# A causal convolution fused with a multiplicative FFN: where two convolution heads stand among the products, and who sums the band matrices

## The chip, the cores and the metric

The kernel runs on 1 core of one Trainium2 chip. The metric is the device time of one execution in microseconds (us). An execution is profiled once, and the trace of that execution is what is read here; times are also taken without the profiler, and their median is the kernel's time. TensorE is called PE (its weight loads PEld), VectorE DVE, ScalarE ACT, GpSimd POOL, SyncE SP.

## What is computed

`x` is (8, 3904, 192). Each of the 8 heads owns 24 of the 192 channels and has 7 taps, a softmax over its row of `weight`. The convolution is causal: output row s is the weighted sum of rows s-6 to s. Its 31232 rows then go through a multiplicative FFN without a nonlinearity:

```python
out_conv = np.einsum('hk,bskhg->bshg', softmax(weight), x_unfolded)
a = x @ w1            # 192 -> 1024
b = x @ w2            # 192 -> 1024
h = a * b @ w3        # 1024 -> 1024
return h @ w_out      # 1024 -> 192
```

## The kernel before

**Two streams.** The rows are cut into two halves of 15616 rows (`NS = 2`), which lie side by side on partitions 0-63 and 64-127. A *round* is 512 rows of each half (`CH = 512`); there are 31 rounds.

**The convolution** (`conv`, L237) works on windows of 64 rows of which 58 are output rows. A window's product with a 64x64 band matrix (`Aband`, seven diagonals that hold a head's taps) is one matmul in a 64x64 tile of PE; four such tiles run side by side. A *block* is up to 36 windows; there are 10 (`SIZES`). A call with `nh = 1` makes one head of one block: two rows of four matmuls into one PSUM buffer (`cps`), which DVE or ACT then copies to `convo`. Blocks 3 to 9 are stored to DRAM (`rows`) and come back as `xT` through transposing DMAs on SP's queue; blocks 0 to 2 are transposed on PE. `conv_two` (L480) makes two heads, with one copying engine each, and calls `store` after the last head.

**The first product** (`first_product`, L345) makes, for each of 8 tiles `ft` of 128 hidden columns, `pa` (x @ w1) and `pb` (x @ w2): six matmuls each, in 64x128 tiles of PE, two side by side. ACT copies `pa` to `asb` (L366), DVE multiplies `asb` by `pb` into `abT` (L367).

**The second product** (`second_product`, L372) multiplies a round's `abT` with `W_sb` = w3 @ w_out (made once, L405 to L420) in 32 matmuls of 128x128 tiles; ACT copies the result (L383), SP stores it. It runs two rounds behind the first.

**PSUM** is one pool of four buffers of two banks (L65). `pa`, `pb`, `cps`, `ops` and the rest take them in turn, so each allocation takes the buffer of the fourth one before it and waits until that one's reader is done.

**The order is written out by hand** (`manual_schedule`, L67); every engine runs its instructions in program order. After a prologue there are 15 phases (L507). Phase 0 has no first product; each later one has two rounds of first product, then two rounds of second product of two halves each: `ops00`, `ops01`, `ops10`, `ops11`. In phases 0 to 11 four heads of a block are made as well: two between `ops00` and `ops01`, two between `ops10` and `ops11`, all copied by DVE (L521). A block thus takes two phases; the even phase makes heads 0 to 3, the odd one heads 4 to 7.

**The prologue** (L135 to L462) loads x and weights, and makes the bands. POOL makes a mask `cmask` (L151), DVE multiplies it by the taps into `cprod` (128 x 2 x 64 x 8, L206), adds the eight taps up in three steps (L213, L216) and copies the two halves of partitions across (L221, with ACT). PE runs 28 dummy matmuls meanwhile (`warm`, L174), then block 0's heads, its transposes and the first round. `wsw` holds the FFN's weights with the two halves of partitions swapped; `swap_w` (L334) makes it in three column parts (0-511, 512-767, 768-1023) for each of three tiles. Part 0 must be there before the first round's `ft` 0, part 1 before `ft` 4, part 2 before `ft` 6. POOL's queue carries the loads of x, w1, w2, w3 and w_out in program order, between its own work.

Of the kernel before, what the change touches and what calls it, by code (L numbers as in the profile page):

```python
# [8 lines left out]

FP32 = mybir.dt.float32  # L10
BF16 = mybir.dt.bfloat16
AX = mybir.AxisListType
ALU = mybir.AluOpType
# [4 lines left out]
def kernel(  # L18
# [10 lines left out]
    nc = tc.nc  # L29

    B, S, D = x.shape
    H, K = weight.shape
# [4 lines left out]
    KP = 8  # L37
    assert K <= KP

    NS = 2  # L40
# [5 lines left out]
    Q = 64  # L46
# [7 lines left out]
    NB = len(SIZES)  # L54
# [7 lines left out]
    const = ctx.enter_context(tc.tile_pool(name="const", bufs=1))  # L62
# [6 lines left out]
    def banks(name):  # L69
        return psum.tile([128, NS, CH], FP32, tag="banks", name=name)  # L70
# [74 lines left out]

    ones = const.tile([128, 1], BF16)
    nc.gpsimd.memset(ones, 1.0)
    cmask = const.tile([128, Q, KP], BF16)
    for r in range(NS):
        ps = slice(Q * r, Q * r + Q)  # L150
        nc.gpsimd.affine_select(  # L151
            out=cmask[ps], in_=ones[ps].unsqueeze(2).to_broadcast([Q, Q, KP]),
            pattern=[[-1, Q], [-1, KP]], compare_op=ALU.is_equal,
            fill=0.0, base=0, channel_multiplier=1)
    wn = [const.tile([128, DFF], BF16, name=f"wn{k}", tag=f"wn{k}") for k in range(3)]
    wsw = [const.tile([128, DFF], BF16, name=f"ws{k}", tag=f"ws{k}") for k in range(3)]

    WC = (0, DFF // 2, DFF * 3 // 4, DFF)

    def load_w(c0, c1):  # L160
        cs = slice(c0, c1)
        nc.gpsimd.dma_start(out=wn[0][:, cs], in_=moe_w1[0:128, cs])
        nc.gpsimd.dma_start(out=wn[2][0:Q, cs], in_=moe_w1[128:192, cs])
        nc.gpsimd.dma_start(out=wn[2][Q:128, cs], in_=moe_w2[128:192, cs])
        nc.gpsimd.dma_start(out=wn[1][:, cs], in_=moe_w2[0:128, cs])

    load_w(0, WC[2])
    ident = const.tile([128, 128], BF16)
    make_identity(nc, ident)

    def warm(n, t=None):
        t = banks("warm") if t is None else t
        for j in range(n):
            nc.tensor.matmul(t[:, j % 2, :], zeros[:, 0:128], zeros, start=True, stop=True)  # L174

    warm(28)


    wmax = const.tile([128, H], FP32)
# [1 line left out]
    wsb = const.tile([128, 2, 2, KP], BF16)  # L181
# [3 lines left out]
        out=wall, in0=wall, in1=wmax.unsqueeze(2).to_broadcast([128, H, K]), op=ALU.subtract)  # L185
# [3 lines left out]
    for r in range(NS):  # L189
        ps = slice(Q * r, Q * r + Q)  # L190
        nc.vector.tensor_tensor(
            out=wsb[ps, :, :, 0:K],
            in0=wall[ps].rearrange("p (g a e) k -> p g a e k", g=2, a=2)[:, :, r],
            in1=wsum[ps].rearrange("p (g a e) -> p g a e", g=2, a=2)[:, :, r].unsqueeze(3)
                .to_broadcast([Q, 2, 2, K]),
            op=ALU.mult)

    Aband = const.tile([128, 2, 2, 2, Q], BF16)
# [2 lines left out]
        g, j, e = h // 4, (h % 4) // 2, h % 2  # L201
        return Aband[Q * r:Q * r + Q, g, int(j != r), e, :]

    def band(g):
        c = slot([128, 2, Q, KP], BF16, "cprod")
        nc.vector.tensor_tensor(  # L206
            out=c,
            in0=cmask.unsqueeze(1).to_broadcast([128, 2, Q, KP]),
            in1=wsb[:, g].unsqueeze(2).to_broadcast([128, 2, Q, KP]),
            op=ALU.mult)  # L210
        n = KP // 2
        while n > 1:
            nc.vector.tensor_tensor(out=c[:, :, :, 0:n], in0=c[:, :, :, 0:n],  # L213
                                    in1=c[:, :, :, n:2 * n], op=ALU.add)
            n //= 2
        nc.vector.tensor_tensor(out=Aband[:, g, 0], in0=c[:, :, :, 0], in1=c[:, :, :, 1],  # L216
                                op=ALU.add)

    def band_swap(g, half, f):
        d, e = ((Q, 0), (0, Q))[half]  # L220
        f(out=Aband[d:d + Q, g, 1], in_=Aband[e:e + Q, g, 0])  # L221


    xT = [const.tile([128, RING], BF16, name=f"xT{k}", tag=f"xT{k}") for k in range(NP)]
# [12 lines left out]
    def conv(b, h0, nh, evict=None, lead=0):  # L237
        n = SIZES[b] // 2
        if h0 == 0:
            convo_of[b] = work.tile([128, n, NP, NS, Q], BF16, tag="convo", bufs=2, name="convo")  # L240
        convo = convo_of[b]
        cps = banks("cps")
        warm(lead, cps)
        wd = nh * G

        def view(ps, r):
            return cps[ps, r, 0:n * wd].rearrange("p (w g) -> p w g", g=wd)

        for j in range(nh):
            h = h0 + j  # L250
            for c in range(2):
                xb, w0 = xb_of[b][c]
                for r in range(NS):
                    nc.tensor.matmul(  # L254
                        view(slice(Q * c, Q * c + Q), r)[:, :, j * G:(j + 1) * G],
                        band_of(h, r),
                        xb[Q * r:Q * r + Q, w0:w0 + n, h * G:(h + 1) * G],
                        start=True, stop=True)
        src = cps[:, :, 0:n * wd].rearrange("p r (w g) -> p r w g", g=wd)
        o, moves = 0, []  # L260
        for k, c0, m in segments(h0 * G, wd):
            moves.append((convo[:, :, k, :, c0:c0 + m].rearrange("p w r g -> p r w g"),
                          src[:, :, :, o:o + m]))
            o += m
        if h0 + nh == H:
            del xb_of[b]
        if evict == ():
            return moves
        for e, (dst, part) in enumerate(moves):
            f = evict or [nc.scalar.copy]  # L270
            f[e % len(f)](out=dst, in_=part)  # L271
# [28 lines left out]
    def pe_transpose(b, k, lead=0):  # L300
        n = SIZES[b] // 2
        convo = convo_of[b]
        tps = banks_bf16("tps")
        for w in range(lead):
            nc.tensor.transpose(out=tps[:, w % 2, :], in_=zeros[:, 0:128], identity=ident)
        for w in range(n):
            nc.tensor.transpose(  # L307
                out=tps[:, w, :],
                in_=convo[:, w, k].rearrange("p r g -> p (r g)"), identity=ident)
        t0 = tok(FIRST[b])  # L310
        dst = xT[k][:, t0:t0 + 2 * n * ST].rearrange("p (c w s) -> p c w s", c=2, w=n)
        src = tps[:, 0:n, :].rearrange("p w (c s) -> p c w s", c=2)
        return dst, src[:, :, :, 0:ST]
# [20 lines left out]
    def swap_w(k, part, engines):  # L334
        cs = slice(WC[part], WC[part + 1])
        for f, (d, e) in zip(engines, ((0, Q), (Q, 0))):
            f(out=wsw[k][d:d + Q, cs], in_=wn[k][e:e + Q, cs])
# [85 lines left out]
    V, A, P = nc.vector.tensor_copy, nc.scalar.copy, nc.gpsimd.tensor_copy  # L423
# [3 lines left out]
    def move(f, pair):  # L427
        f(out=pair[0], in_=pair[1])  # L428

    band(0)  # L430
    band_swap(0, 0, V)
    band_swap(0, 1, A)
    band(1)
    band_swap(1, 0, V)
    m0, m1 = conv(0, 0, 4, ())
    move(A, m0)
    band_swap(1, 1, A)
    move(V, m1)
    t0 = pe_transpose(0, 0, 10)
    swap_w(0, 0, (V, A))  # L440
    for m in conv(0, 4, 2, ()):
        move(V, m)
    for m in conv(0, 6, 2, ()):
        move(A, m)
    move(V, t0)
    swap_w(2, 0, (V, A))
    t1 = pe_transpose(0, 1, 8)
    move(V, t1)
    t2 = pe_transpose(0, 2)
    move(A, t2)  # L450
    swap_w(1, 0, (V, A))
    for k in (0, 2, 1):
        swap_w(k, 1, (P, V))
    load_w(WC[2], WC[3])
    load_x(2)
    for k in (0, 2, 1):
        swap_w(k, 2, (P, P))
    load_wo()
# [5 lines left out]
    def seq(*fs):  # L464
        def run():
            for f, *a in fs:
                f(*a)
        return run

    first_product(0, lead=2, between={  # L470
        2: seq((conv, 1, 0, 4)),
        3: seq((conv, 1, 4, 4)),
        6: seq((pe_transposes, 1))})
    first_product(1, {
        0: seq((conv, 2, 0, 4)),
# [4 lines left out]
    def conv_two(b, h, engines):  # L480
        for j, f in enumerate(engines):
            conv(b, h + j, 1, (f,))
        if h + 2 == H:
            store(b)

    def send(last):
        while sent[0] <= last and min((sent[0] + 1) * CH, TS) <= stored[0]:
            transposes(sent[0])
            sent[0] += 1
# [16 lines left out]
    done = 0  # L506
    for p, rounds in enumerate(phases):  # L507
        b, e = PROLOGUE_BLOCKS + p // 2, p % 2
        if b < NB:
            for xb, r, w in zero_rows.pop(b, []):  # L510
                nc.gpsimd.memset(xb[Q * r:Q * r + PAD, w, :], 0.0)
        for j, R in enumerate(rounds):
            first_product(R)
            if j == 0 and b + 1 < NB:
                P(out=pace, in_=abT_of[R][0:1, JT - 1, 1, 0:2])  # L515
                load_x(b + 1, (0, 1) if p == 1 else (e,))
        last = NR if p == len(phases) - 1 else done + 2
        for i in range(done, last):
            second_product(i, 0)
            if b < NB and i < done + 2:  # L520
                conv_two(b, 4 * e + 2 * (i - done), (V, V))  # L521
            second_product(i, 1)
        done = last
        send(min(NR - 1, LAG + 2 * p + 4))
    assert sent[0] == NR

# [29 lines left out]
```

## Time and profile before

| | |
|---|---|
| median of 3 runs | 532.54 us (532.4 to 532.62) |
| the profiled execution | 533.68 us, its span 532.0 us |
| PE busy | 524.0 us (98% of the span) |
| DVE, ACT, POOL busy | 363.1 us, 317.4 us, 53.0 us |
| chain that ended last | PE 94%, DVE 3%, ACT 1%, DMA 1% |
| first product, L360 | 59% of the span on that chain |
| second product, L378 | 31% |
| convolution heads, L254 | 2% |
| first matmul of round 0 | 14.02 us after the span's start |
| a phase with heads | 106.8 to 139.5 us (first product to 127.6) |
| a phase without heads | 464.9 to 496.5 us |

The span is the time from the first to the last instruction of the trace; the rest of an execution's time lies around it. A group of instructions has its line in the source, its engine, its operation and its tiles (`out<-in`). Waits are given with the engine that waits and the instruction that ended the wait. The matmuls of one row of tiles run side by side, so the distance from one start to the next, and not their own lengths, tells what PE needs for them.

### The profile page before, as it was taken

To read this page: it belongs to the slowest core of one execution; us is meant where nothing else is said; L and a number is where in the kernel's file an instruction comes from. 1 tells how busy PE (TensorE), PEld (TensorE's weight loads), DVE (VectorE), ACT (ScalarE), POOL (GpSimd) and SP (SyncE) were. 2 spreads that over 40 slices of the span, in tenths; PEclk is the share of its full clock that TensorE was granted. 3 is DMA by queue.
4 is the path that set the end of the run, shared out by engine and by line. 5 is a ranking of instruction groups with operands and counts; after the bars stand their busy time and mean duration, and the time that the engine had idled before them with its cause. 6 is when DMAs were issued, how large, how long until landed. Compare 5 with 4: busy or idle time off the path is not lost.

```text
span 532.0 us, 12708 instructions
## 1 busy us (share of the span) xinstructions
PE 524.0 (98%) x5469; PEld 339.3 (64%) x5469; DVE 363.1 (68%) x350; ACT 317.4 (60%) x350; POOL 53.0 (10%) x95
## 2 busy tenths in 40 slices
PE   8999999999999999999999999999999999999995
PEld 4455874846658476584765757557575674847685
DVE  6779459578594875949669496784957849286560
ACT  3888647375573755737467374664746647375552
POOL 8851002002010100201001010020000000000000
PEclk9999999999999999999999999999999999999998
DMA  7999457989473694637956468655624065240203
GB/s 101 141 206 182 93 96 171 206 175 125 132 99 99 154 144 129 88 103 156 137 139 78 130 150 128 118 66 145 136 80 120 1 172 106 90 76 31 90 22 130
DMA packets 130541, 63.13 MB, mean 119 GB/s; under 512 B 83352, under 2 KB 129460, under 8 KB 130484
## 3 DMA queue, kind: packets, MB, share of 16 engines
q1 hardware_dynamic: 91764, 45.65, 35.7%
q0 software_dynamic: 38576, 16.63, 26.3%
q8 instruction: 43, 0.70, 0.6%
q14 instruction: 14, 0.11, 0.1%
q10 hardware_dynamic: 144, 0.03, 0.0%
HBM read 33.28 MB, written 34.82 MB: 128 GB/s over the span
## 4 chain that ended last, share of the span: by engine, by line
PE 94%; DVE 3%; ACT 1%; DMA 1%; issue 0%; ACTq 0%; DVEq 0%
PE ops L378 31%; PE pa L360 30%; PE pb L360 29%; PE cps L254 2%; DVE abT L367 1%; PE wps L418 1%; ACT asb L366 1%; DMA wall<-in_weight_dram 1%; PE tps L307 1%; PE w3ps L409 0%; DVE cprod L213 0%; DVE cprod L206 0%; DVE Aband L216 0%; DVE convo L428 0%; DVE w3T L412 0%
## 5 line engine op out<-in xcount | busy, mean ns | idle before, releaser
L367 DVE TENSOR_TENSOR abT<-asb,pb 128x1024 bf16<-128x1024 bf16 (+1 forms) x248 | 298.4, 1204 | 77.0 <-ACT asb L366 60.5
L366 ACT CAST asb<-pa 128x1024 bf16<-128x1024 f32 (+1 forms) x248 | 247.6, 999 | 64.1 <-PE pa L360 63.4
L360 PE MATMUL pb<-xT,wn 64*128 64x512 bf16 (+1 forms) x744 | 199.7, 373 | 0.2
L360 PE MATMUL pa<-xT,wn 64*128 64x512 bf16 (+1 forms) x744 | 197.8, 373 | 0.4
L360 PE MATMUL pa<-xT,ws 64*128 64x512 bf16 (+1 forms) x744 | 197.9, 373 | 0.0
L360 PE MATMUL pb<-xT,ws 64*128 64x512 bf16 (+1 forms) x744 | 195.7, 373 | 0.0
L360 PEld LDWEIGHTS <-wn 64*128 64x128 bf16 x1488 | 138.3, 94 | 84.6 <-issue 2.6
L360 PEld LDWEIGHTS <-ws 64*128 64x128 bf16 x1488 | 130.3, 94 | 72.0 <-issue 1.4
L378 PEld LDWEIGHTS <-abT 128*128 128x128 bf16 x1952 | 159.1, 98 | 13.8 <-issue 13.8
L378 PE MATMUL ops<-W_sb,abT 128*128 128x192 bf16 x1952 | 167.8, 246 | 0.0
L383 ACT COPY osb<-ops 128x768 f32<-128x768 f32 (+1 forms) x62 | 48.9, 789 | 134.1 <-PE ops L378 134.1
L271 DVE CAST convo<-cps 128x864 bf16<-128x864 f32 (+7 forms) x65 | 52.0, 847 | 66.7 <-PE cps L254 66.7
L111 POOL DMA_DIRECT2D xb<-in_x_dram x38 | 29.9, 797 | 12.2 <-DMA w3b<-in_moe_w_dram 5.2
L515 POOL COPY pace<-abT 1x2 bf16<-1x2 bf16 x9 | 1.6, 176 | 269.7 <-DVE abT L367 269.7
L254 PE MATMUL cps<-xb,Aband 64*64 64x432 bf16 (+3 forms) x320 | 17.8, 309 | 0.2 <-DVE abT L367 0.2
L174 PE MATMUL warm<-zeros 128*128 128x512 bf16 x28 | 8.9, 491 | 1.4 <-DVE wsb L182 1.4
L254 PEld LDWEIGHTS <-Aband 64*64 64x64 bf16 x320 | 5.8, 105 | 6.8 <-issue 5.7
L271 ACT CAST convo<-cps 128x640 bf16<-128x640 f32 (+4 forms) x13 | 7.4, 606 | 0.8 <-PE cps L254 0.8
L174 PEld LDWEIGHTS <-zeros 128*128 128x128 bf16 x30 | 3.4, 119 | 6.5 <-issue 3.6
L418 PE MATMUL wps<-wo_b,w3T 128*128 128x192 bf16 x64 | 6.3, 246 | 0.1
L418 PEld LDWEIGHTS <-w3T 128*128 128x128 bf16 x64 | 5.1, 98 | 1.0 <-issue 1.0
L409 PE MATMUL w3ps<-ident,w3b 128*128 128x128 bf16 x64 | 4.6, 219 | 0.0
(55 smaller groups left out, 64.3 us busy)
## 6 DMA issues: line engine op xcount, KB each, us to landing
out_dram<-osb SPq DMA_DIRECT2D x60, 384.0 KB, 2.9
xb<-in_x_dram POOLq DMA_DIRECT2D x14, 432.0 KB, 8.9
rows<-convo SPq DMA_DIRECT2D x7, 648.0 KB, 7.5
xb<-in_x_dram POOLq DMA_DIRECT2D x8, 384.0 KB, 9.9
w3b<-in_moe_w_dram POOLq DMA_DIRECT2D x8, 256.0 KB, 8.8
rows<-convo SPq DMA_DIRECT2D x3, 576.0 KB, 8.4
xT<-rows SPq DMA_TRANSPOSE x84, 2.7
rows<-convo SPq DMA_DIRECT2D x2, 540.0 KB
```

What stands on the lines that cost most here:

```text
L111: nc.gpsimd.dma_start(out=xb[Q * r:Q * r + Q, w:w + m, :], in_=x_spans(r, i, m))
L174: nc.tensor.matmul(t[:, j % 2, :], zeros[:, 0:128], zeros, start=True, stop=True)
L254: nc.tensor.matmul(view(slice(Q * c, Q * c + Q), r)[:, :, j * G:(j + 1) * G], band_of(h, r), xb[Q * r:Q * r + Q, w0:w0 + n, h * G:(h + 1) ...
L271: f[e % len(f)](out=dst, in_=part)
L307: nc.tensor.transpose(out=tps[:, w, :], in_=convo[:, w, k].rearrange("p r g -> p (r g)"), identity=ident)
L360: nc.tensor.matmul(p[:, r, 0:N], w_of(i, k, r)[rs, ft * 128:(ft + 1) * 128], xT[k][rs, r0:r0 + N], start=(k == 0), stop=(k == NP - 1))
L366: nc.scalar.copy(out=asb[:, :, 0:N], in_=pa[:, :, 0:N])
L367: nc.vector.tensor_tensor(out=ab[:, ft, :, 0:N], in0=asb[:, :, 0:N], in1=pb[:, :, 0:N], op=ALU.mult)
L378: nc.tensor.matmul(ops[:, g // 2, (g % 2) * D:(g % 2) * D + D], ab[:, jt, r, g * 128:(g + 1) * 128], W_sb[:, jt, :], start=(jt == 0), stop ...
L383: nc.scalar.copy(out=osb.rearrange("p (a g) d -> p a (g d)", g=2), in_=ops[:, 0:ng // 2, 0:2 * D])
L409: nc.tensor.transpose(out=tps[:, gt, :], in_=w3b[:, gt * 128:(gt + 1) * 128], identity=ident)
L418: nc.tensor.matmul(wps[:, 0, 0:D], w3T[:, gt, :], wo_b[:, gt, :], start=(gt == 0), stop=(gt == JT - 1))
```

## The change

Three things are changed.

1. **The phases.** Two heads come right behind the first product, ahead of `ops00`, copied by ACT and DVE; two come behind `ops11`, ahead of the next phase's first product, copied by DVE. The four second products stand together. With it, `store` moves behind `ops11`.
2. **The bands.** `band_taps` keeps the multiplication by the taps; its mask is now one diagonal, read with overlapping windows of 8. `band_sum` adds the taps up on PE: seven matmuls with an identity into PSUM for the straight band and seven with a swapped identity for the other, 128 columns each that are 8 elements (16 bytes) apart; one copy per group (ACT, DVE) takes both. DVE's adds and the four copies across go away. POOL makes the identities (128x128 and 128x64) and the diagonal (two of 64x72) in place of two masks of 64x512, and the later identity.
3. **The rest of the prologue.** 16 dummy matmuls in place of 28, none among the transposes; block 0's heads in four calls of two; `swap_w` moves mostly to POOL (tiles 0 and 2 of part 0, all of part 1; only tile 1 of part 0 stays with DVE and ACT); the loads of the later weight columns and of x come at other places of POOL's queue. In round 0 the second half of block 1's heads moves from behind `ft` 3 to behind `ft` 4.

```diff
-    cmask = const.tile([128, Q, KP], BF16)
-    for r in range(NS):
-        ps = slice(Q * r, Q * r + Q)
+    identw = const.tile([128, 128 + Q], BF16)
+    diag = const.tile([128, Q + KP], BF16)
+    for m in (identw[:, 0:128], identw[:, 128:128 + Q], diag[0:Q], diag[Q:128]):
+        p, n = m.shape
         nc.gpsimd.affine_select(
...
+    ident, swapped = identw[:, 0:128], identw[:, Q:Q + 128]
...
-    ident = const.tile([128, 128], BF16)
-    make_identity(nc, ident)
...
-    warm(28)
+    warm(16)
...
-    def band(g):
+    d0 = diag[:, 0:1]
+    taps = bass.AP(tensor=d0.tensor, offset=d0.offset,
+                   ap=[list(d0.ap[0]), [0, 2], [1, Q], [1, KP]])
+
+    def band_taps(g):
         c = slot([128, 2, Q, KP], BF16, "cprod")
         nc.vector.tensor_tensor(
...
+            out=c, in0=taps, in1=wsb[:, g].unsqueeze(2).to_broadcast([128, 2, Q, KP]),
             op=ALU.mult)
...
+    def band_sum(g, c, f):
+        bps = banks("bps")
+        for v, lhsT in enumerate((ident, swapped)):
+            out = bps[:, 0, v * 128:v * 128 + 128].rearrange("p (e s) -> p e s", e=2)
+            for k in range(K):
+                nc.tensor.matmul(out, lhsT, c[:, :, :, k], start=(k == 0), stop=(k == K - 1))
+        f(out=Aband[:, g].rearrange("p v e s -> p (v e s)"), in_=bps[:, 0, 0:256])
...
+    c0, c1 = band_taps(0), band_taps(1)
+    band_sum(0, c0, A)
+    band_sum(1, c1, V)
+    for h, f in ((0, V), (2, A), (4, V), (6, A)):
+        for m in conv(0, h, 2, ()):
+            move(f, m)
+    swap_w(0, 0, (P, P))
+    swap_w(2, 0, (P, P))
+    load_w(WC[2], WC[3])
+    for k, f in ((0, V), (1, A), (2, V)):
+        move(f, pe_transpose(0, k))
     swap_w(1, 0, (V, A))
+    load_x(2)
     for k in (0, 2, 1):
-        swap_w(k, 1, (P, V))
-    load_w(WC[2], WC[3])
-    load_x(2)
+        swap_w(k, 1, (P, P))
...
-        3: seq((conv, 1, 4, 4)),
+        4: seq((conv, 1, 4, 4)),
...
+        if b < NB:
+            conv_two(b, 4 * e, (A, V))
         last = NR if p == len(phases) - 1 else done + 2
         for i in range(done, last):
             second_product(i, 0)
-            if b < NB and i < done + 2:
-                conv_two(b, 4 * e + 2 * (i - done), (V, V))
             second_product(i, 1)
         done = last
+        if b < NB:
+            conv_two(b, 4 * e + 2, (V, V))
         send(min(NR - 1, LAG + 2 * p + 4))
```

More of the change, by code (lines that the diff above doesn't have):

```diff
@@ L6 @@
 from concourse import bass_utils, mybir
-from concourse.masks import make_identity
 from concourse._compat import with_exitstack
@@ L147 @@
     nc.gpsimd.memset(ones, 1.0)
-    cmask = const.tile([128, Q, KP], BF16)
-    for r in range(NS):
-        ps = slice(Q * r, Q * r + Q)
+    identw = const.tile([128, 128 + Q], BF16)
+    diag = const.tile([128, Q + KP], BF16)
+    for m in (identw[:, 0:128], identw[:, 128:128 + Q], diag[0:Q], diag[Q:128]):
+        p, n = m.shape
         nc.gpsimd.affine_select(
-            out=cmask[ps], in_=ones[ps].unsqueeze(2).to_broadcast([Q, Q, KP]),
-            pattern=[[-1, Q], [-1, KP]], compare_op=ALU.is_equal,
-            fill=0.0, base=0, channel_multiplier=1)
+            out=m, in_=ones[0:p].to_broadcast([p, n]), pattern=[[-1, n]],
+            compare_op=ALU.is_equal, fill=0.0, base=0, channel_multiplier=1)
+    ident, swapped = identw[:, 0:128], identw[:, Q:Q + 128]
     wn = [const.tile([128, DFF], BF16, name=f"wn{k}", tag=f"wn{k}") for k in range(3)]
@@ L202, in band_of @@
         return Aband[Q * r:Q * r + Q, g, int(j != r), e, :]
-    def band(g):
+    d0 = diag[:, 0:1]
+    taps = bass.AP(tensor=d0.tensor, offset=d0.offset,
+                   ap=[list(d0.ap[0]), [0, 2], [1, Q], [1, KP]])
+    def band_taps(g):
         c = slot([128, 2, Q, KP], BF16, "cprod")
         nc.vector.tensor_tensor(
-            out=c,
-            in0=cmask.unsqueeze(1).to_broadcast([128, 2, Q, KP]),
-            in1=wsb[:, g].unsqueeze(2).to_broadcast([128, 2, Q, KP]),
+            out=c, in0=taps, in1=wsb[:, g].unsqueeze(2).to_broadcast([128, 2, Q, KP]),
             op=ALU.mult)
[L211 to L221, printed above, removed]
+        return c
+    def band_sum(g, c, f):
[5 more added lines that the diff above has]
+        f(out=Aband[:, g].rearrange("p v e s -> p (v e s)"), in_=bps[:, 0, 0:256])
     xT = [const.tile([128, RING], BF16, name=f"xT{k}", tag=f"xT{k}") for k in range(NP)]
@@ L428, in move @@
         f(out=pair[0], in_=pair[1])
[L430 to L450, printed above, removed]
+    c0, c1 = band_taps(0), band_taps(1)
[9 more added lines that the diff above has]
+        move(f, pe_transpose(0, k))
     swap_w(1, 0, (V, A))
+    load_x(2)
     for k in (0, 2, 1):
-        swap_w(k, 1, (P, V))
-    load_w(WC[2], WC[3])
-    load_x(2)
+        swap_w(k, 1, (P, P))
     for k in (0, 2, 1):
```

## The prediction

> **What bounds the kernel now.** I read the page first: busy shares, then the chain that ended last.
>
> ```profile
> PE 524.0 (98%) x5469; PEld 339.3 (64%) x5469; DVE 363.1 (68%) x350; ACT 317.4 (60%) x350; POOL 53.0 (10%) x95
> ...
> PE 94%; DVE 3%; ACT 1%; DMA 1%; issue 0%; ACTq 0%; DVEq 0%
> ```
>
> PE holds the end. The waits that are listed for it add up to 1.6 us, of which 0.2 lie behind the dummy matmuls, so a change can take away PE's own overhead, or add a wait. Next the timeline at the border of a phase, PE alone:
>
> ```profile
> 127.08 0.38 PE L360 MATMUL pb<-xT,wn 64*128 64x512 bf16 x1
> 127.29 0.38 PE L360 MATMUL pb<-xT,ws 64*128 64x512 bf16 x1
> 127.30 0.38 PE L360 MATMUL pb<-xT,wn 64*128 64x512 bf16 x1
> 127.61 2.81 PE L378 MATMUL ops<-W_sb,abT 128*128 128x192 bf16 x32
> 130.35 0.56 PE L254 MATMUL cps<-xb,Aband 64*64 64x432 bf16 x8
> ```
>
> Pairs of `pb` start 0.21 apart, but `ops` starts 0.31 behind the last pair: PE pays about 0.095 whenever the tile shape changes (64x128, 128x128, 64x64), and the new shape's second matmul comes 0.01 late. I take 0.105 per change of shape. DVE at the same border, then the one place where a head had to wait:
>
> ```profile
> 125.52 2.52 DVE L367 TENSOR_TENSOR abT<-asb,pb 128x1024 bf16<-128x1024 bf16 x2
> ```
>
> ```profile
> 51.09 1.22 DVE L367 TENSOR_TENSOR abT<-asb,pb 128x1024 bf16<-128x1024 bf16 x1
> 52.36 0.36 PE L254 MATMUL cps<-xb,Aband 64*64 64x384 bf16 x4 [0.24 <-DVE abT L367]
> ```
>
> The first row's second product (`ft` 6) ends at 128.04, 0.43 after PE has left the first product; all eleven borders of phases 1 to 11 lie at 0.43. The second pair shows what a buffer that DVE still reads costs: PE starts 0.05 after DVE's end.
>
> **The phases: shapes.** A phase with two rounds changes shape six times (first product, ops, heads, ops, heads, ops, first product); phase 0 five times. Afterwards each has four. 11 x 2 + 1 = 23 changes at 0.105: **-2.4 us**. The matmuls themselves stay. No trace of before shows heads between 64x128 products without a wait except in the prologue, where the change costs the same 0.09.
>
> **The phases: wait A.** PSUM buffers go in turn, four of them. At the new border the first head takes the buffer of `pa` 6 (ACT done long ago); the second takes that of `pb` 6, which DVE reads until 0.43 behind the border, so PE may write it at 0.43 + 0.05 = 0.48. Without a wait it would start one row of four matmuls later, at 0.20. Wait 0.28; today `ops00`'s 2.7 us hide it. Behind the waiting head stand all of `ops`, so nothing hides it now. `ops00` itself needs `pa` 7's buffer, which ACT leaves in time (127.06 + 1.01 = 128.08). 11 borders x 0.28 = **+3.1 us**. Phase 0 has no first product ahead of it.
>
> **The phases: wait B.** The last two heads now stand directly ahead of the next first product, both copied by DVE. Today's second pair of heads and the next first product:
>
> ```profile
> 136.23 0.56 PE L254 MATMUL cps<-xb,Aband 64*64 64x432 bf16 x8
> 136.72 2.81 PE L378 MATMUL ops<-W_sb,abT 128*128 128x192 bf16 x32
> 139.47 0.39 PE L360 MATMUL pa<-xT,wn 64*128 64x512 bf16 x1
> ```
>
> ```profile
> 136.66 2.09 DVE L271 CAST convo<-cps 128x576 bf16<-128x576 f32 x3 [3.78 <-PE cps L254]
> ```
>
> From the heads' start, DVE is done 2.52 later (0.43 + 2.09; 2.45 where no head is split). The first product would start 0.49 behind the heads, its second `pb` 1.95 after that (139.47 to 141.42): at 2.44. It takes the second head's buffer, the fourth before it, free at 2.57 or 2.50: waits of 0.13 (even phases) and 0.06 (odd). For the phases 0 to 9 that is 5 x 0.13 + 5 x 0.06 = **+0.9 us**; the heads of phases 10 and 11 have 15 windows, and DVE is done in time. The next `pb` needs the first product of DVE, which can then start at 2.52 and is done at 3.74, 0.07 ahead. ACT's new share, one head of about 0.9 behind `asb`, falls into 2.7 us without other work (its wait ahead of `osb` is 2.38). `store` comes some 3 us later on SP, behind all output stores instead of three; the transposes behind it feed rounds two phases later, over 30 us away.
>
> **The prologue.** Today round 0's first `pb` stands until ACT's swap of weights is done:
>
> ```profile
> 14.36 0.62 ACT L337 COPY ws<-wn 64x512 bf16<-64x512 bf16 x1
> 15.03 0.10 PEld L360 LDWEIGHTS <-ws 64*128 64x128 bf16 x2 [0.47 <-ACT ws L337]
> ```
>
> The new chain to the same matmul, by rows: the taps' product stays at 0.69 on DVE (L206; the bounds are 0.69 and the 1.22 that DVE takes for the same 1024 results in L367, which would cost 0.5 here), so the two groups are there at 7.43 and 8.13. The 16th dummy matmul ends its turn at 7.50 (the 14th starts at 6.85, at full clock they stand 0.216 apart). Then 28 band matmuls. Their price isn't shown, since no matmul here reads columns 16 bytes apart. These rows lie on both sides:
>
> ```profile
> 8.36 0.38 DVE L216 TENSOR_TENSOR Aband<-cprod 128x128 bf16<-128x128 bf16 x1
> ```
>
> ```profile
> 10.51 0.73 PE L305 MATMUL tps<-ident,zeros 128*128 128x128 bf16 x10
> ```
>
> Ten dense 128-column matmuls take 0.73, (0.73 - 0.22) / 9 = 0.056 each: the lower bound. DVE's last add reads the same tile at the same distance: 0.38 less about 0.16 of fixed time (0.692 for 1024 results in L206 and 0.428 for 512 in L213 leave 0.16) is 0.22 per 128 results: the upper bound, if PE gets a column as seldom. Each of those results reads two elements, 0.11 per 128 reads. I take **0.11**, half the dense rate: it uses the row of the same tile, charged per read. 28 x 0.11 = 3.1: the last starts at 10.47, its result is there at 10.7. DVE's copy of 256 columns (L428: 0.49 for 320) ends at 11.15; heads 4 to 7 follow on PE. DVE copies heads 0, 1 (480 columns, about 0.65) and 4, 5 (0.71, as at 12.36) until 12.43, ACT heads 6, 7 about then. PE transposes tile 1 from 12.48, result 12.95; ACT copies it (0.64) until 13.65 and swaps weights (0.62) until 14.28; `pb` goes on at 14.33, not 15.03: **-0.7 us**. At 0.056 the same chain gives -2.2 (the swap ends at 12.7), at 0.22 it gives +2.3 (27 intervals of 0.11 more).
>
> In a sentence of its own: the Trainium skill (SBUF — State Buffer, Specifications) says that SBUF lines are 16 bytes, that full bandwidth needs two hits per line, and that each new line costs a penalty. By it, as an estimate, the dense price falls out and the total lies between +0.9 and +3.9; the row of L216 agrees, as far as a read by DVE can.
>
> POOL's four selects take some 0.95 (0.29 for 128 columns, 2.1 ns per column by the masks' 1.1 for 512) in place of 2.2, so the weight loads leave 1.2 us earlier. Its swaps of 512 columns cost about 0.62 (0.40 for 256, 0.18 for the 2 columns of `pace`); the four are done at 11.6, long before 13.5. Then four loads, one x pair (1.49), six swaps at 0.46: done at 18.05, where `ft` 4 needs them at about 19.4; part 2 at 20.8, needed at 22.5. They hide behind `ft` 0 to 3; without that cover a late swap stops PE one to one. The w3 loads leave 1.1 us later than 20.6, and PE first needs them at 50.6. Block 1's heads behind `ft` 4: the same two ACT copies, zero.
>
> **Sum**: -2.4 + 3.1 + 0.9 - 0.7 = **+0.9 us**. On the profiled execution (533.68; span 532.0, 1.7 around it) 534.6; the median of runs lies 1.14 lower, so **533.4**. What a measurement of this kernel can tell from no change is about 0.2%, 1.07 us.
>
> **Rivals.**
> - *Dense bands* (0.056). For: the adds into PSUM and the weight loads are as for transposes. Against: L216. -2.4 + 3.1 + 0.9 - 2.2 = -0.6: 531.9.
> - *Slow bands* (0.22 each). For: L216 whole. Total +3.9: 536.4, slower. It decides from about 0.12 per matmul on.
> - *No wait A*: the gain of shapes remains. If the second head got a buffer that is free (another turn than one in four), or its copy began earlier, -2.4 + 0.9 - 0.7 = -2.2, without wait B too -3.1: 529.4 to 530.3, faster. For: PE shows no such waits today. Against: the turn of four follows from the code, and 52.36 shows this very wait.
> - *The clock falls in the prologue*: the dummy matmuls among the transposes go, and PE has gaps. Today the spacing of dummy matmuls halves (0.427 to 0.216) at 6.8 and stays so. A second slow stretch as long as the first (1.39 to 6.8, 5.4 us) would do half its work: +2.7 on the forecast, 536.1. Against: no gap in the chain above is over 1 us. In a sentence of its own: the Trainium skill (TensorE: Matmul & The Clock Gate, What's actually happening) lets the clock fall only after an idle window of about 3.4 us, and by that rule it wouldn't fall here; no run here shows such a fall yet.
>
> **How the numbers follow.** Chances: forecast 0.36 (its own range 532.9 to 534.2), dense 0.25, slow 0.22, no wait A 0.09, clock 0.08. Range 531.7 to 536.9: it leaves out no wait A and the tails. Faster by over 0.2%: 0.11 (no wait A, a little of dense). Within: 0.45 (dense, and 0.6 of the forecast, which lies near the limit of 533.6). Slower: 0.44 (slow, clock, the rest).
>
> **What would show it.** At eleven borders the second head should start 0.48 behind the first, not 0.20, 0.05 after the end of an `abT`; the second `pb` of a phase should start 2.5 to 2.57 behind the last heads; a phase should last 0.1 to 0.2 longer than its 32.69 (106.84 to 139.53 on the chain). The band matmuls' spacing and the start of round 0's first `pb` (14.3) test the prologue. I am wrong if PE waits on POOL's swaps, if the first heads of a phase wait for x, or if the clock's row shows a second dip.

## The result, and the profile after

The changed kernel takes **537.79 us** (median of 4 runs, 537.35 to 538.74) beside 532.47 us for the kernel before (4 runs, 532.36 to 532.62): ratio 1.0102, 95% interval 1.0085 to 1.012. It is slower by 5.3 us. The forecast was 533.4, its range 531.7 to 536.9. The profiled execution took 538.74 us, its span 537.0.

The page of the changed kernel: busy time of the engines, the row of the granted clock in 40 slices, and the group of the band matmuls (L218). The last line is the clock's row of the kernel before.

```profile
PE 528.6 (98%) x5467; PEld 353.6 (66%) x5467; DVE 346.7 (65%) x326; ACT 326.2 (61%) x360; POOL 54.8 (10%) x102
...
PEclk9799999999999999999999999999999999999999
...
L218 PE MATMUL bps<-cprod,identw 128*128 128x128 bf16 x28 | 6.5, 407 | 0.0
```

```profile
PEclk9999999999999999999999999999999999999998
```

The second slice of the clock's row is a 7, where the kernel before has a 9, and 28 small matmuls occupy PE for 6.5 us. PE is as busy as before; the work in it has become longer. Where does the time come in? I followed the starts of each phase's first `pa` through both traces:

| | before | after | difference |
|---|---|---|---|
| first matmul of w3's stage | 50.58 | 54.43 | +3.85 |
| phase 1's first product | 74.09 | 77.83 | +3.74 |
| phase 3 | 139.47 | 143.59 | +4.12 |
| phase 7 | 270.22 | 275.09 | +4.87 |
| phase 12 | 433.42 | 439.19 | +5.77 |
| last matmul | 526.39 | 532.16 | +5.77 |

So the prologue brings +3.85 (forecast -0.7) and the phases bring +1.9 (forecast -2.4 + 3.1 + 0.9 = +1.6). The span grew by 5.0 only, since what follows the last matmul took 4.9 instead of 5.6.

**The prologue.** PE in the timeline of the changed kernel (start, length of the stretch, engine, line, operation):

```profile
6.91 6.55 PE L218 MATMUL bps<-cprod,identw 128*128 128x128 bf16 x28
13.39 1.20 PE L252 MATMUL cps<-xb,Aband 64*64 64x120 bf16 x32
14.66 1.76 PE L305 MATMUL tps<-identw,convo 128*128 128x128 bf16 x15
...
18.46 0.63 PE L358 MATMUL pb<-xT,wn 64*128 64x512 bf16 x1
```

The bands stand 0.2275 apart (first start 6.914, last 13.057), not 0.11. The 15 transposes take 1.76, 0.107 each, twice the 0.056 of dense ones in the kernel before. The first `pb` starts at 18.46; forecast 14.33 for its swapped half. The clock, in windows of PE (from and to, length, busy time and matmuls, then the granted clock, the DMA share and GB/s), first before, then after:

```profile
9.02:12.43 3.41, 3.27 (x58) 1.00 1.09 156
12.43:15.85 3.42, 3.30 (x34) 1.00 1.31 154
15.85:19.25 3.40, 3.32 (x44) 1.00 1.14 116
```

```profile
9.02:12.43 3.41, 3.41 (x17) 1.00 1.09 141
12.43:15.85 3.42, 3.35 (x49) 0.50 1.11 126
15.85:19.25 3.40, 3.40 (x18) 0.50 1.23 145
19.25:22.66 3.41, 3.34 (x44) 1.00 0.13 9
```

A *window* of the clock is 3.41 us here: in every trace the stretches between two changes of the clock are whole multiples of it (6.82 us in this one; 3.41, 10.24 and 17.07 in x4_strides below). In the window ahead of the fall PE is occupied for all of its 3.41 us, by band matmuls alone. Then two windows of half clock follow.

**The border of a phase.** PE and then DVE inside phase 2, where its first product ends; the second head is shown from a stretch of its own, because the timeline otherwise joins both heads into one row:

```profile
131.33 0.38 PE L358 MATMUL pb<-xT,wn 64*128 64x512 bf16 x1
131.64 0.38 PE L252 MATMUL cps<-xb,Aband 64*64 64x432 bf16 x4
...
132.12 0.38 PE L252 MATMUL cps<-xb,Aband 64*64 64x432 bf16 x4
```

```profile
130.85 1.22 DVE L365 TENSOR_TENSOR abT<-asb,pb 128x1024 bf16<-128x1024 bf16 x1
```

The second head starts 0.48 behind the first and 0.05 behind DVE's end (130.85 + 1.22 = 132.07): wait A, as forecast. The list of waits doesn't name it, since the modelled end of the first head (132.02) covers most of it; the starts show it.

**The first product behind the last heads**, PE and DVE at the start of phase 3:

```profile
145.33 0.38 PE L358 MATMUL pa<-xT,ws 64*128 64x512 bf16 x1
145.66 0.37 PE L358 MATMUL pb<-xT,wn 64*128 64x512 bf16 x1
```

```profile
143.52 2.08 DVE L269 CAST convo<-cps 128x576 bf16<-128x576 f32 x3 [9.19 <-PE cps L252]
```

The second `pb` should follow 0.216 behind the last `pa` pair; it follows 0.33 behind it, 0.05 after DVE's end (145.60): wait B. Of the three things that the prediction named as signs of being wrong, the clock's second dip came. POOL is no bound: its swaps of part 0 are done at 11.5, and PE nowhere waits for them. Nor do the first heads of a phase wait for x: at all eleven borders they start 0.306 behind the last `pb`, as `ops` did before the change (0.308).

### The profile page after: what moved, and what is told of

The parts are those of the page before. It is cut to its first block, busy times and chain, and to the rows that moved or that the text cites. A ratio compares the mean times of both kernels' runs of the same rounds, so it can differ in the third digit from the quotient of the medians.

```text
span 537.0 us, 12707 instructions
## 1 busy us (share of the span) xinstructions
PE 528.6 (98%) x5467; PEld 353.6 (66%) x5467; DVE 346.7 (65%) x326; ACT 326.2 (61%) x360; POOL 54.8 (10%) x102
## 4 chain that ended last, share of the span: by engine, by line
PE 91%; DVE 4%; ACT 3%; issue 1%; ACTq 0%
PE ops L376 30%; PE pa L358 28%; PE pb L358 26%; DVE abT L365 4%; ACT asb L364 3%; PE cps L252 2%; PE bps L218 1%; PE wps L416 1%; PE warm L172 1%; PE tps L305 1%; PE w3ps L407 0%; PE pa L172 0%; ACT convo L269 0%; DVE w3T L410 0%; ACT osb L381 0%
## 5 line engine op out<-in xcount | busy, mean ns | idle before, releaser
L358 PE MATMUL pb<-xT,wn 64*128 64x512 bf16 (+1 forms) x744 | 201.8, 373 | 0.2
L376 PE MATMUL ops<-W_sb,abT 128*128 128x192 bf16 x1952 | 163.7, 246 | 0.0
L269 DVE CAST convo<-cps 128x864 bf16<-128x864 f32 (+8 forms) x53 | 40.6, 805 | 112.8 <-PE cps L252 112.8
L252 PE MATMUL cps<-xb,Aband 64*64 64x432 bf16 (+3 forms) x320 | 20.3, 320 | 1.5 <-DVE abT L365 0.2
L269 ACT CAST convo<-cps 128x864 bf16<-128x864 f32 (+6 forms) x25 | 17.7, 727 | 1.1 <-PE cps L252 0.8
L252 PEld LDWEIGHTS <-Aband 64*64 64x64 bf16 x320 | 7.2, 109 | 13.7 <-issue 12.9
L335 POOL COPY ws<-wn 64x256 bf16<-64x256 bf16 (+1 forms) x16 | 7.2, 449 | 0.8
L172 PE MATMUL warm<-zeros 128*128 128x512 bf16 x16 | 5.7, 533 | 1.4 <-DVE wsb L180 1.4
L218 PE MATMUL bps<-cprod,identw 128*128 128x128 bf16 x28 | 6.5, 407 | 0.0
```

The source lines that it names most:

```text
L218: nc.tensor.matmul(out, lhsT, c[:, :, :, k], start=(k == 0), stop=(k == K - 1))
L252: nc.tensor.matmul(view(slice(Q * c, Q * c + Q), r)[:, :, j * G:(j + 1) * G], band_of(h, r), xb[Q * r:Q * r + Q, w0:w0 + n, h * G:(h + 1) ...
L358: nc.tensor.matmul(p[:, r, 0:N], w_of(i, k, r)[rs, ft * 128:(ft + 1) * 128], xT[k][rs, r0:r0 + N], start=(k == 0), stop=(k == NP - 1))
L376: nc.tensor.matmul(ops[:, g // 2, (g % 2) * D:(g % 2) * D + D], ab[:, jt, r, g * 128:(g + 1) * 128], W_sb[:, jt, :], start=(jt == 0), stop ...
```

## The experiments

All times are medians; the kernel before, on the same chips, had 532.41 to 532.57.

| run | what it is | us | ratio to before, 95% interval |
|---|---|---|---|
| x1_phases | before, new phases only | 534.63 | 1.0045 (1.0032 to 1.0057) |
| x2_prologue | before's phases, new prologue | 536.03 | 1.0070 (1.0058 to 1.0083) |
| x3_dense | after, dense bands | 532.56 | 1.0002 (0.9993 to 1.0011) |
| x5_dense_oldphases | dense bands, before's phases | 531.17 | 0.9968 (0.9955 to 0.9980) |
| x6_half | after, bands 8 bytes apart | 533.58 | 1.0017 (1.0008 to 1.0027) |
| x7_wait_a | before, first pair of heads moved | 534.67 | 1.0042 (1.0029 to 1.0054) |
| x8_wait_b | before, second pair moved | 532.27 | 0.9992 (0.9983 to 1.0001) |
| x9_best | x5, second pair moved, DVE and ACT copy | 531.69 | 0.9985 (0.9976 to 0.9994) |
| x11_half_cold | x6, spread dummy matmuls | 533.57 | 1.0018 (1.0009 to 1.0027) |
| x12_half_twice | x6, bands made twice | 536.66 | 1.0081 (1.0067 to 1.0094) |

My theory after the result: the phases cost what was forecast (waits A and B less the shapes), and the rest comes from the bands' reads, twice: by their own length and by the clock that falls behind them. The rivals: the phases cost more than their trace shows; the clock falls for another reason (the dummy matmuls that went, gaps).

### Each half alone

x1_phases, in the kernel before:

```diff
+        if b < NB:
+            conv_two(b, 4 * e, (A, V))
...
-            if b < NB and i < done + 2:
-                conv_two(b, 4 * e + 2 * (i - done), (V, V))
...
+        if b < NB:
+            conv_two(b, 4 * e + 2, (V, V))
```

> Only the new order of the phases, on the kernel before; its prologue is kept. Theory: in the changed kernel's trace the phases 1 to 11 lose 0.15 to 0.22 us each (first product of phase 1 is 3.74 late, of phase 12 5.77), since the second head's wait of 0.29 and the second pb's wait of 0.12 or 0.06 outweigh two changes of tile shape at 0.105. So about +1.9 on 532.5: 534.4. Rival: the loss lies in the prologue alone, and the phases gain their changes of shape: 530 to 532.5. What tells: the ratio, and the distance of the two rows of heads at the border (0.47 against 0.20).

x2_prologue is the changed kernel with that edit taken back.

> Only the new bands and the new prologue; the phases have the old order. Theory: the prologue keeps its loss of about 3.8 us (28 band matmuls at 0.229 and a clock that falls at 12.4), and the phases lose nothing: 532.5 + 3.6 = 536.0. Rival (the phases are the bulk): 533 to 534.

Measured: +2.2 and +3.6 on the 532.42 of before; together 5.8, of which the whole change shows 5.3. In x2_prologue the bands again stand 0.2276 apart, and the clock is at half from 10.88 to 17.70. Both halves are slower by themselves, each about as its trace says.

### Dense bands

```diff
-                   ap=[list(d0.ap[0]), [0, 2], [1, Q], [1, KP]])
+                   ap=[list(d0.ap[0]), [1, K], [0, 2], [1, Q]])
...
-        c = slot([128, 2, Q, KP], BF16, "cprod")
+        c = slot([128, K, 2, Q], BF16, "cprod")
...
-                nc.tensor.matmul(out, lhsT, c[:, :, :, k], start=(k == 0), stop=(k == K - 1))
+                nc.tensor.matmul(out, lhsT, c[:, k], start=(k == 0), stop=(k == K - 1))
```

> The changed kernel with the taps' product laid out tap by tap, so that a band matmul reads its 128 columns densely; DVE's product then has its 7 x 128 elements with one operand constant along a row. Theory (the price of columns 16 bytes apart): the 28 matmuls take 0.056 each, DVE's product between 0.75 and 1.2, and the first pb's swapped half starts near 13 instead of 18.5; 537.8 - 5 = 532.5 to 533, the clock falls later or not at all. Rival (POOL's swaps, the order of the copies or the fewer dummy matmuls make the loss): 536 or more, with the first pb still at 17 or later.

Measured 532.56, 5.2 less than the changed kernel, with full clock until the last matmul. The bands take 1.73 from the first to the last start, though DVE now needs 1.09 per taps' product instead of 0.75. POOL's swaps, the order of the copies and the 16 dummy matmuls are the changed kernel's, so they don't make the loss. The distance of the columns makes the whole loss of the prologue. With the old phases as well:

> The changed kernel's prologue with the taps' product laid out tap by tap (the bands' matmuls read dense columns), and the order of the phases from before. Theory: the two halves of the change add up, so the dense prologue alone is worth x3_dense less x1_phases, 532.56 - 534.63 = -2.1 us against before: 530.2 to 530.7, clock 1.00, below both kernels. Rival (the dense prologue's gain is an accident of when the weights' DMA landed, or of the later phases starting earlier): 531.8 or more.

Measured 531.17: faster than both kernels, by 0.32% than before (0.20 to 0.45%). The gain is 1.4, less than the 1.8 to 2.3 that the expectation gives, and below the 531.8 of its rival; in the profiled executions the last matmul comes 1.71 earlier (524.68, 526.39).

### What a distance between columns costs

```diff
+    spread = const.tile([128, 32 * 128], BF16)
+    nc.vector.memset(spread, 0.0)
+    for step, n in ((1, 16), (2, 16), (4, 16), (8, 16), (16, 16), (32, 16), (1, 32), (8, 64)):
+        t = banks("probe")
+        for j in range(n):
+            nc.tensor.matmul(t[:, j % 2, 0:128], zeros[:, 0:128],
+                             spread[:, 0:128 * step].rearrange("p (c s) -> p c s", s=step)[:, :, 0],
+                             start=True, stop=True)
```

> The kernel before with 192 more matmuls on zeros behind the 28 dummies (128 columns each; 16 each with columns 1, 2, 4, 8, 16 and 32 elements apart, then 32 dense ones, then 64 with 8 apart), whose results nobody uses. It measures the disputed price by itself. Theory: the price goes with the 16-byte lines that a matmul touches: 0.056 at 1, and about 0.229 at 8, 16 and 32 alike, with 2 and 4 between or dense. Rivals: the price grows on with the distance (16 at 0.46), or every distance over 1 costs the same. The clock: if it follows the columns that PE takes, it falls in the 14.7 us of the 64 spread matmuls though PE never idles; if it follows occupancy, it stays full. The time itself grows by some 25 us and says nothing.

x10_rates has the same loop with (4, 128), (1, 128), (6, 64), (1, 128), (5, 80).

> The kernel before, with probe matmuls of 128 columns of zeros between the dummy matmuls and the rest: 128 at 4 elements apart (14.7 us, four whole windows of the clock), 128 dense, 64 at 6 elements apart, 128 dense, 80 at 5 elements apart. Its time is not compared. Theory: spacings of 0.115 at 4 elements, 0.14 to 0.18 at 5 and 6 (between the 0.115 and 0.227 that x4_strides gave for 4 and 8), and dense ones 0.056 or 0.107. The clock: if it goes by the columns taken, it falls in the stretch at 6 elements, and perhaps already in the one at 4 (half of the columns); where it holds over two whole windows at 4, half of the columns is enough. Rival (only what stands 16 bytes or more apart lowers the clock): it holds in all three.

Start to start, for one matmul of 128 columns of 2 bytes (the two runs agree where they share a distance):

| elements apart | 1 | 2 | 4 | 5 | 6 | 8 | 16 | 32 |
|---|---|---|---|---|---|---|---|---|
| us | 0.056 | 0.057 | 0.115 | 0.143 | 0.171 | 0.227 | 0.233 | 0.218 |

128 columns at distance s span 128 x 2s / 16 = 16s lines of 16 bytes up to s = 8, and 128 lines beyond. At 0.227 for 128 lines a line costs 1.77 ns; that gives 0.114, 0.142 and 0.170 for s = 4, 5 and 6, as measured. Beyond s = 8 the price no longer grows with the distance; that 0.233 and 0.218 differ from 0.227 by up to 4% is not explained. At s = 2 (32 lines, 0.057) the columns themselves cost as much. The price at s = 8 is 0.227 at full clock and at half: it isn't PE's clock that sets it.

And the clock, in windows of PE in x4_strides. The matmuls at 8, 16 and 32 elements run from 13.80 to 24.4, dense ones to 27.7, then those at 8 again:

```profile
10.35:13.77 3.42, 3.42 (x48) 1.00 1.19 142
13.77:17.18 3.41, 3.41 (x17) 1.00 1.04 122
17.18:20.59 3.41, 3.41 (x16) 0.50 1.26 137
...
24.00:27.42 3.42, 3.42 (x31) 0.50 1.16 209
27.42:30.83 3.41, 3.41 (x22) 1.00 1.12 208
30.83:34.24 3.41, 3.41 (x17) 0.50 1.11 207
```

In x10_rates those at 4 elements run from 10.0 to 24.7, dense ones to 31.9, those at 6 to 42.8, dense ones to 50.6, those at 5 to 61.9:

```profile
16.82:20.23 3.41, 3.41 (x32) 1.00 1.31 148
20.23:23.65 3.42, 3.42 (x32) 1.00 0.75 75
...
33.90:37.32 3.42, 3.42 (x22) 1.00 1.49 192
37.32:40.74 3.42, 3.42 (x22) 0.50 1.60 191
...
50.97:54.39 3.42, 3.42 (x26) 1.00 0.00 0
54.39:57.80 3.41, 3.41 (x26) 0.50 0.00 0
```

PE is occupied in every one of these windows. The clock falls behind each whole window that holds only matmuls at 8, 6 or 5 elements (a quarter, 0.33 and 0.39 of the dense columns), and holds over whole windows at 4 (0.056 / 0.1155 = 0.48). Dense ones bring it back after a window. So neither gaps nor missing dummy matmuls are needed for a fall, and the rival that only 16 bytes or more count is wrong too: at 5 elements the columns are 10 bytes apart. That the clock goes by the columns that PE takes in a window, and not by something that goes with them, is the simplest reading of these rows; they don't show it by themselves.

The ends of the kernels bear it out from the other side, with dense matmuls and idle time. The last matmuls of the kernel before, and the stretch after them:

```profile
525.60:529.01 3.41, 1.04 (x13) 1.00 0.70 232
529.01:531.98 2.97, 0.00 (x0) 0.50 0.03 6
```

PE works for 1.04 of the 3.41 us, by the modelled ends of its matmuls, a share of 0.30, and the clock falls behind that window without a whole idle one. In x8_wait_b it falls behind a last window with 1.32 us of work (0.39); in x3_dense it holds behind one with 1.47 (0.43). So a window partly idle and a window full of slow matmuls turn at about the same share.

### The forecast's own price

x6_half lays the taps' product out in two halves of four taps, so that columns are 4 elements apart:

```diff
-        c = slot([128, 2, Q, KP], BF16, "cprod")
+        c = slot([128, 2, 2, Q, KP // 2], BF16, "cprod")
...
-                nc.tensor.matmul(out, lhsT, c[:, :, :, k], start=(k == 0), stop=(k == K - 1))
+                nc.tensor.matmul(out, lhsT, c[:, k // 4, :, :, k % 4], start=(k == 0), stop=(k == K - 1))
```

> The changed kernel, with the taps' product in two halves of four taps, so that the bands' matmuls read columns 4 elements (8 bytes) apart instead of 8. x4_strides gave 0.115 us per matmul at that distance, nearly the 0.11 that the forecast took; so this is the forecast's own prologue. Theory (only the price of the band matmuls, and the clock that follows from it, was wrong): the band matmuls stand 0.115 apart, the clock stays at 1.00 (x4_strides kept full clock in a window that was half such matmuls, half dense ones), and the time is the forecast's, 533.0 to 534.0. Rival (the clock falls whenever PE streams below full rate for a whole window of 3.4 us): half clock for about 3.4 to 6.8 us in the prologue, 534.5 to 535.5.

Measured 533.58, the forecast's 533.4 nearly; the clock stays full, so the rival of the expectation falls, and the prologue goes as forecast:

```profile
7.74 3.42 PE L222 MATMUL bps<-cprod,identw 128*128 128x128 bf16 x28
...
14.55 0.52 PE L362 MATMUL pb<-xT,ws 64*128 64x512 bf16 x2
```

The swapped half of the first `pb` starts at 14.55, forecast 14.33, of which 0.24 is that the bands start at 7.74 and not at 7.50. Only the price of a band matmul, and what hangs on it, was wrong in that chain.

### The price of the half clock

x11_half_cold, in x6_half, was to keep the clock low without making the bands longer (`spread` is a tile of 1024 zeros):

```diff
-            nc.tensor.matmul(t[:, j % 2, :], zeros[:, 0:128], zeros, start=True, stop=True)
+            nc.tensor.matmul(t[:, j % 2, 0:128], zeros[:, 0:128],
+                             spread.rearrange("p (c s) -> p c s", s=8)[:, :, 0],
+                             start=True, stop=True)
```

> x6_half, with the 16 dummy matmuls reading 128 zeros 16 bytes apart (0.227 us each in x4_strides) in place of 512 dense ones (0.216 each at full clock), so that PE is occupied for as long but takes a quarter of the columns. The bands stay at 8 bytes. Theory (the clock goes by the columns that PE takes in a window of 3.4 us, not by whether it has work): the clock stays at half until about 17 us, the band matmuls still stand 0.115 apart, and what the half clock costs in the prologue alone shows: 1.0 to 2.0 us over x6_half, 534.6 to 535.6, clock about 0.98 to 0.99. Rival (the clock rises when PE is occupied, as the zero gaps suggest): as x6_half, 533.3 to 534.0, clock 1.00.

Measured 533.57, as x6_half: my expectation failed. The clock did stay at half longer, until 10.77 instead of 7.28, but not until 17: the bands at 4 elements (0.116 each, near the 0.107 of dense ones at half clock) raised it. Until then nothing on PE depended on the clock. So this run says nothing on the price; it only shows that spread dummy matmuls raise the clock later than dense ones, and a part of that may lie with PE's 1.4 us without work ahead of the bands.

x12_half_twice turns it round: as long a stretch of bands as in the changed kernel, at full clock.

```diff
-            for k in range(K):
+            for k in 2 * list(range(K)):
```

> x6_half, with each sum of seven band matmuls made twice (the second starts anew), so that 56 of them at 0.116 occupy PE for 6.5 us, as the changed kernel's 28 at 0.2275 do, but take twice the columns. x10_rates held full clock for whole windows of such matmuls. Theory (the changed kernel pays for the length of the bands and, apart from it, for the half clock that they bring): full clock throughout, 533.58 + 28 x 0.116 = 536.8 at most, 535.8 to 536.9, and what the changed kernel has above it (537.79) is the price of the half clock, 1 to 2 us. Rival (the half clock costs nothing, since other engines set the pace there; all of the 4.2 us between x6_half and the changed kernel is the bands' length): 537.4 to 538.5.

Measured 536.66 (536.46 to 537.29). Its bands occupy PE as the changed kernel's do, and the clock stays:

```profile
6.98 6.69 PE L222 MATMUL bps<-cprod,identw 128*128 128x128 bf16 x56
```

```profile
12.43:15.85 3.42, 2.99 (x59) 1.00 0.87 104
15.85:19.25 3.40, 3.40 (x32) 1.00 1.18 124
```

The changed kernel has 537.79, 1.1 more. In the profiled executions the first `pb` comes at 16.98 here and at 18.46 there, though its bands end 0.3 later: 1.8; the last matmuls lie 1.78 apart (530.38, 532.16). So the half clock costs 1.1 to 1.8, and the bands' length (533.58 to 536.66) about 3.1. The rival, that it costs nothing, falls. The low clock did not last equally long in each run: the mean granted clock of the changed kernel is 0.991 in the profiled execution (538.74), 0.994 at 537.88, and 0.997 at 537.69 and 537.35. As an estimate from these means, that is some 9 us at half clock in the first, the stretch behind the last matmul included, and some 3 in the last two. So 1.8 belongs to a long stretch of half clock, and 1.1 to the median run, whose stretch was shorter.

### Each wait alone

x7_wait_a and x8_wait_b move one pair of heads each, in the kernel before:

```diff
+        if b < NB:
+            conv_two(b, 4 * e, (A, V))
...
-            if b < NB and i < done + 2:
+            if b < NB and i == done + 1:
```

> The kernel before, with only the first pair of heads of a phase moved to the border behind the first product (ACT and DVE copy); the second pair stays between ops10 and ops11. Theory (the second head waits for DVE's read of the last pb): 11 borders x 0.31 (0.29 of wait, and 0.02 that the ops behind it start later) less 12 changes of shape x 0.1 = +2.2 us: 534.4 to 534.9, and 0.29 of excess ahead of every second head. Rival (the waits of the new order lie with the last pair of heads, ahead of the next first product): 531.3 to 532.3.

```diff
-            if b < NB and i < done + 2:
+            if b < NB and i == done:
...
+        if b < NB:
+            conv_two(b, 4 * e + 2, (V, V))
```

> The kernel before, with only the second pair of heads of a phase moved behind ops11, ahead of the next first product (both copied by DVE); the first pair stays between ops00 and ops01. Theory: ten waits of the second pb for DVE's copy, 5 x 0.13 + 5 x 0.06 = +0.9, less 12 changes of shape x 0.1 = -1.2: -0.3 us, 531.9 to 532.5. Rival (the last pair costs the phases their time): 533.5 or more.

Measured 534.67 (+2.1) and 532.27 (-0.26; the interval just takes in no change). In x7_wait_a each second head starts 0.485 behind the first, 0.053 after DVE's end. In x8_wait_b the second `pb` of a phase starts 0.336 or 0.272 behind the pair ahead of it, for 0.216 without a wait: 0.12 and 0.056, as forecast (0.13 and 0.06). The loss of the phases is wait A. So I tried to keep the shapes' gain of the second pair and drop its wait:

> x5_dense_oldphases, with the second pair of heads of a phase moved behind ops11 and copied by DVE and ACT (in x8_wait_b DVE copies both). Theory: 12 changes of shape less and no wait of the second pb, since ACT copies its buffer while DVE copies the first head: 12 x 0.1 = -1.2 us against x5_dense_oldphases, 529.8 to 530.3, and the lowest of all kernels here. Rival (ACT's copy comes behind osb of ops11 and the waits stay, or move to the next asb): 530.8 or more.

Measured 531.69, not below x5_dense_oldphases (531.17): the rival of the expectation. ACT at that place, then PE:

```profile
104.64 0.80 ACT L383 COPY osb<-ops 128x768 f32<-128x768 f32 x1 [1.84 <-PE ops L378]
105.34 0.88 ACT L271 CAST convo<-cps 128x864 bf16<-128x864 f32 x1
106.11 2.09 ACT L366 CAST asb<-pa 128x1024 bf16<-128x1024 f32 x2
```

```profile
108.06 0.38 PE L360 MATMUL pa<-xT,ws 64*128 64x512 bf16 x1
108.45 0.37 PE L360 MATMUL pb<-xT,wn 64*128 64x512 bf16 x1
```

ACT works without a pause from `osb` through the head to the first `asb`; DVE's `abT` follows, and the third `pb` waits for its buffer 0.053 beyond DVE's end (108.395): 0.168 late. That is more than the 0.12 or 0.06 of wait B and the 0.095 of the change of shape. A phase lasts 32.76 instead of 32.69. The wait went from one copying engine to the other.

## Why the prediction was wrong

- **The band matmul, the step that failed.** The prediction bounded it between 0.056 and 0.22, took 0.11 "charged per read" from DVE's add, and measured is 0.2275: 27 x (0.2275 - 0.11) = +3.2. The row of L216 had the right number whole (0.22 per 128 results); dividing it by two reads was a choice that no row supported. Whether DVE and PE pay this price for the same reason, no run shows. The sentence on the Trainium skill (SBUF — State Buffer, Specifications) pointed to the right end. The Trainium skill asks there for at least two hits per line for full bandwidth, and two were not enough here: at 8 bytes apart, two columns per line, PE ran at half rate (0.115), and at 4 bytes, four per line, at full rate (0.057).
- **The clock.** The rival had the chance 0.08 on the ground that no gap in the chain was over 1 us. There was no such gap, and the clock fell. The Trainium skill (TensorE: Matmul & The Clock Gate, What's actually happening) lets it fall after an idle window of some 3.4 us; the length agrees (3.41 us and its multiples), but the clock fell behind windows that slow matmuls occupied throughout. The prediction's "no run here shows such a fall yet" missed the end of the trace before, where the clock falls behind a window with 1.04 us of work. Its price was put at +2.7; measured 1.1 to 1.8.
- **Two rivals that were one.** Slow bands (536.4) and the fall of the clock (536.1) stood side by side as if each excluded the other. The first brings the second: 28 x 0.2275 = 6.4 us are nearly two windows of 3.41, so most often a whole one lies inside. Added up, 536.4 + 1.1 to 1.8 gives 537.5 to 538.2; measured 537.79. The range ended at 536.9.
- **Shapes, waits A and B: right.** +1.6 forecast, +1.9 in the changed kernel's trace, +2.2 in x1_phases. Each change of shape costs 0.09 to 0.095 from start to start, and 0.10 by the sum of the phases, (3.1 + 0.26 + 0.9 - 1.9) / 23, where 0.105 was taken; each second head waits 0.29 (0.28 forecast), each second `pb` 0.12 or 0.056. What was missing is 0.024 more on the `ops` behind the waiting head (0.299 instead of 0.275), 0.26 over 11 borders.
- **The rest of the prologue: right.** x6_half, whose bands cost nearly the forecast's 0.11, has 533.58 where 533.4 was forecast. POOL's work hid, the heads of block 1 behind `ft` 4 cost nothing to see, and the taps' product took 0.75 with overlapping windows (0.69 taken). In the profiled execution of the changed kernel the bands began at 6.91, not 7.50, since the convolution's weights landed 0.7 earlier than in that of before. Together: -0.7 + 3.2 + 1.8 - 0.6 = +3.7, beside the +3.85 of the table.

## What to carry to other kernels

Price a matmul's moving operand by the 16-byte lines that it touches as well as by its columns: a layout that is handy for the engine that writes it can make PE's reads four times as long, and laying the product out tap by tap turned this change's prologue from +3.6 into a gain. Where work is moved between stages, write down whose buffer each instruction takes and when that one's reader is done; the 0.29 per border and its source were to be had from the trace of before. And ask of each rival whether it brings another one about; then the case is their sum.

## What the runs showed of the hardware

- PE needs some 1.77 ns for each 16-byte line of a partition that its moving operand touches: 128 columns take 0.218 to 0.233 us where each lies in a line of its own, and at 16 bytes apart 0.227 at full and at half clock; dense columns take 0.056 and 0.107.
- PE's clock falls to half though PE is never without a matmul: behind windows of 3.41 us with 0.39 or less of the dense columns. At 0.48 it held over three whole windows. Dense matmuls for 0.39 of a window and idle time for the rest let it fall (x8_wait_b), for 0.43 not (x3_dense).
- A wait of PE for a PSUM buffer can be missing from the list of waits, where the modelled end of the matmul ahead covers it; the distance between starts shows it (0.48 instead of 0.19).
